# Overlapping weights of the dilated heads added before the ones matmuls, q and k loads moved ahead of half of the value loads, and the query and key copies of two batches moved

## The chip, the cores and the metric

The kernel runs on one core of one Trainium2 chip. The metric is the device time of one execution in microseconds (us), as the median of the runs taken. The engines named below are PE (TensorE, the matmuls), DVE (VectorE), ACT (ScalarE), POOL (GpSimd) and SP (SyncE); in this kernel POOL mostly issues the loads and SP mostly the transposing DMAs and the stores.

## What is computed

Windowed attention over 8 batches, 8 heads, 576 positions and 64 features, followed by a feed-forward layer over the 4608 tokens. Heads 0 to 3 ("near") look at the last 32 positions; heads 4 to 7 ("dilated") look at every fourth of the last 128.

```python
scores = q @ k.transpose(0, 1, 3, 2) / sqrt(64)
rel = pos[:, None] - pos[None, :]
near    = (rel >= 0) & (rel < 32)                        # heads 0..3
dilated = (rel >= 0) & (rel < 128) & (rel % 4 == 0)      # heads 4..7
attn = softmax(where(mask, scores, -1e9))
x = (attn @ v) laid out as [4608, 512]
h = maximum(x @ w_in, 0)          # [4608, 2048]
out = (h * h) @ w_out             # [4608, 512]
```

## The kernel before

**Groups.** The feed-forward layer is cut into 288 groups, numbered from 0. The first 64 groups do the first 1024 tokens in tiles of 256; after that each tile of 512 tokens has 32 groups. The first 16 groups of such a tile are the first layer (line 888: four matmuls of 512 columns each into one PSUM tile `pf`, which ACT then empties with a Relu at line 901 and DVE squares at line 902). The last 16 are the second layer (line 930, four matmuls a group, one `pf` tile for four groups, which ACT copies out at line 936). The pool `ps_f`, whose tiles are named `pf`, has four buffers; `ps_a` (`pa`) has two, `ps_o` (`po`) and `ps_d` (`pd`) one each.

**Attention between the groups.** The attention of later batches is put between the groups by a list that is written out by hand: entries (group, rank, batch, code), sorted by group and rank and carried out after that group. The engines run their instructions in program order, so this list sets the order on PE, ACT and DVE. Batch b is tied to group t = 32(b-1). The heads of a batch are taken as four pairs e = 0 to 3; e = 0 and 1 are near, e = 2 and 3 dilated. The codes are:

- R (line 475 on): DVE copies the 16 first and 16 last positions of the dilated heads of a batch into `ends`, which lies in the tile `kbd`; four codes, two copies each (lines 479 and 482).
- K and Q (lines 471 and 473): copies of keys into `k_both` (in `kbd`) and of queries into `q_both` (the tile `qT`); for batches 5 to 7 there are four K and four Q codes for e = 0 and as many for e = 1. A code that ends in "a" runs on ACT, any other on DVE.
- V: a *visit*, the function `quadrants`. It takes a list of pairs whose scores are wanted and a list of pairs whose softmax weights are ready, and issues all their matmuls (line 617) as 64 by 64 pieces, on the four quadrants of the PE array at once. Each piece goes to the quadrant (g, c): row half g, column half c. The order of issue is made by always taking from the quadrant that has the fewest columns so far.
- E: exponential of one half of a pair's scores on ACT (line 654), then the mask on DVE (line 656). For near pairs two adds (line 663) then put sums of overlapping columns into `sums`, in `kbd`.
- L and X: logarithm of the denominators (lines 630 and 631, or 635 and 636) and exponential of its negative (line 640) on ACT, then two multiplications on DVE that write the attention output `xT` (lines 643 and 645).

**One visit.** For each pair with weights there are the products with v (the list `P_` in the code) and the products with a block of ones (the list `D_`), which give the denominators. For a dilated pair each row half has 8 pieces of 80 and 2 of 64 columns in `P_` (768 columns), and 4 pieces of 160 and 2 of 64 in `D_` (768 columns). In `D_`, the two chunks x = 0 and 1 of a residue class cover positions 0 to 79 and 48 to 127, so they overlap in 48 to 79. For a near pair, a row half has 832 columns in `P_` and 608 in `D_`. Scores are 384 columns a quadrant for a dilated pair, and 448 or 384 for a near one.

With one pair, `P_` and `D_` of a row half lie in different quadrants. With two pairs (a *double* visit) `P_` and `D_` of one pair lie in the same quadrant, and the other pair has the other two quadrants. The second pair of a double visit takes two `pf` tiles for its outputs and denominators, and the second pair of scores takes two more.

Visits that hold a dilated pair's weights are these: group 59 (pairs 2 and 3 of batch 2 together), groups 71, 81 and 101 (one dilated pair each), and seven double visits with one near and one dilated pair, at groups 119, 143, 151, 175, 183, 207 and 215. For batch 6, whose t is 160, the visit at group 151 makes the scores of its pair 0; for batch 7 it is the visit at group 183.

**Loads.** POOL issues the loads in order. For batches 4 to 7 the order is: `load_v_rows(b, "d0")`, then four loads of q and k of batch b+1 (two of 320 KB, two of 256 KB), then `load_v_rows(b, "1")`. The "d" part is eight loads (the values of the dilated heads), "0" and "1" are eight loads of 18 KB each for the near pairs 0 and 1. The q and k tiles are then turned by four DMA transposes (line 238) from SP. A load of q into a staging tile waits until the transposes of the batch before have read it.

**Where the copies stand.** For batch 6 the R codes follow groups 134 to 137, the K and Q codes for pair 0 groups 137 to 143, all on DVE; for batch 7 it is 32 groups later. For batch 5 the R codes are at 109 to 112 and K and Q of pair 0 at 112 to 116, with Q on ACT.

Of the kernel before, what the change touches and what calls it, by code (L numbers as in the profile page):

```python
# [27 lines left out]
    "1o0 1o1f | 1a3 1Q0 | 1K0 1o3 | 1Q1 1K1 | 1Q2 | 1b0 | | 1Q3 1K2 L2:vwp L3:q00123 L3:q10123 L2:vwdr | L2:x | | "  # L28
    "2q0 | | 2k0 1V2 | 1b2 1p0 | 1b1 1V3 1K3 | L3:x | 1p2 1p1f | 2a0 1b3 | 2k1l 2b0 2o0 1p3f 2k1h | 2q1 | | 2p0 "
    "L3:Vd0 L4:q00123 L4:q10123 L3:V1 2a1 | 2b1 | | 2o1 | | | 2p1f | | | | L4:x | | | | | | | | | | | | | | | | | "  # L30
    "| L4:Vd0 L5:q10123 L5:q00123 L4:V1 | | | | | | | | | | | | | | | | L5:x | L5:Vd0 L6:q10123 L6:q00123 L5:V1"
)


# [29 lines left out]
def kernel(  # L64
# [258 lines left out]
    def scores(b: int, e: int, part: int):  # L323
        ps = ps_a.tile([P, 512], f32, name="pa")
        if part == 0:
            pts[e] = p_pool.tile([P, 832], bf16, name="pt")
        pt = pts[e]
        n = 0
        for i, r, m0, m1 in blocks(b, e, part):
            if r is None:  # L330
                w = RES * (m1 - m0)
                nc.tensor.matmul(  # L332
                    ps[:, n : n + w].rearrange("p (r m) -> p r m", r=RES),
                    kbd[:, e, i, :], qT[:, e, :, m0:m1], start=True, stop=True,
                )
            else:
                w = m1 - m0
                nc.tensor.matmul(ps[:, n : n + w], kbd[:, e, i, :], qT[:, e, r, m0:m1], start=True, stop=True)
            n += w
        off, mask = half_at(b, e)  # L340
        off *= part
        nc.scalar.activation(pt[:, off : off + n], ps[:, 0:n], ACT.Exp, scale=SCALE)
        nc.vector.tensor_tensor(
            out=pt[:, off : off + n], in0=pt[:, off : off + n],
            in1=mask[:, off : off + n], op=ALU.mult,
        )
# [138 lines left out]
            )  # L485

    sums = kbd[:, 3, 0:4, :].rearrange("p (e x) c -> p e (x c)", e=2)
    sp, op = {}, {}

    def byr(ap):  # L490
# [2 lines left out]
    def quadrants(scs, pvs):  # L493
# [14 lines left out]
        for n, (b, e) in enumerate(pvs):  # L508
# [11 lines left out]
            for g, rows in enumerate(sides):  # L520
# [9 lines left out]
                if not dil:  # L530

                    def blk(i):
                        y = 448 * (i % 2) + 96 * (i // 2)
                        return byr(w[:, y : y + (64 if i == 8 else 96)])

                    for x, i0, k in ((1, 1, 4), (0, 2, 3)):
                        for i in range(i0, i0 + 2 * k, 2):
                            P_.append((o4[:, :, 16 * i - 16 : 16 * i + 8], vrow(i), blk(i), 96))
                        y, m0 = 448 * x + 96 * (i0 // 2), 24 - 16 * x
                        to = d4.rearrange("p r (i m) -> p i r m", m=32)  # L540
                        mid = w[:, y : y + 96 * k].rearrange("p (i r m) -> p i r m", i=k, r=RES)
                        D_.append((to[:, 0:k, :, m0 : m0 + 8], one, mid[:, :, :, 8:16], 32 * k))
                        m0 = 16 * x
                        k = 4 - x
                        pairs = sums[rows, e, 128 * x : 128 * x + 32 * k].rearrange("p (i r m) -> p i r m", i=k, r=RES)
                        D_.append((to[:, 0:k, :, m0 : m0 + 8], one, pairs, 32 * k))
                    for i, ms, to, z in ((0, slice(16, 24), slice(0, 8), 32), (0, slice(0, 16), None, 64), (8, slice(0, 16), slice(112, 128), 64)):
                        P_.append((end if to is None else o4[:, :, to], vrow(i), blk(i)[:, :, ms], z))
                        if to is None or i:
                            D_.append((dend if to is None else d4[:, :, to], one, blk(i)[:, :, ms], z))  # L550
                    D_.append((d4[:, :, 112:120], one, blk(7)[:, :, 16:24], 32))
                else:
                    for x in range(2):
                        ms = slice(48 * x, 48 * x + 80)
                        for j in range(2):
                            y = 448 * (j ^ turn_)
                            piece = w[:, y : y + 320].rearrange("p (c m) -> p c m", c=2)[:, :, 80 * x : 80 * x + 80]
                            for c in range(2):
                                r = 2 * c + j
                                P_.append((o4[:, r, ms], vds[b][rows, e - NE // 2, x, D * r : D * r + D], piece[:, c, :], 80))  # L560
                            D_.append((d4[:, j::2, ms], one, piece, 160))
                    for i, j, to in ((0, 1, None), (8, 0, slice(112, 128))):
                        y = 448 * (j ^ turn_) + 320
                        P_.append((end if to is None else o4[:, :, to], vrow(i), byr(w[:, y : y + 64]), 64))
                        D_.append((dend if to is None else d4[:, :, to], one, byr(w[:, y : y + 64]), 64))
# [53 lines left out]
    def natural_step(b: int, code: str):  # L619
# [28 lines left out]
        else:  # L648
            g = int(code[2])
            if g == 0:  # L650
                pts[b, e] = p_pool.tile([P, 832], bf16, name="pt")
            n = 384 if e >= NE // 2 else (448, 384)[g]
            pt = pts[b, e][:, 448 * g : 448 * g + n]
            nc.scalar.activation(pt, sp[b, e][g][:, 0:n], ACT.Exp, scale=SCALE)  # L654
            mask = (mask_f if e >= NE // 2 else mask_n)[:, 0:n]
            nc.vector.tensor_tensor(out=pt, in0=pt, in1=mask, op=ALU.mult)  # L656
            if g and e < NE // 2:
                even, odd = (
                    pts[b, e][:, y : y + 384].rearrange("p (i r m) -> p i r m", i=4, r=RES) for y in (0, 448)
                )  # L660
                for x, one, two in ((0, even, odd), (1, odd[:, 0:3], even[:, 1:4])):
                    n = 4 - x
                    nc.vector.tensor_tensor(
                        out=sums[:, e, 128 * x : 128 * x + 32 * n].rearrange("p (i r m) -> p i r m", i=n, r=RES),
                        in0=one[:, :, :, 16:24], in1=two[:, :, :, 0:8], op=ALU.add,
                    )
# [19 lines left out]
    def first_step(code: str):  # L686
# [56 lines left out]
        elif what == "S":  # L743
# [2 lines left out]
                first["S", e, part] = pool.tile([P, 512], f32, name=nm)  # L746
            ps = first["S", e, part]
            if part == 0:
                pts[e] = p_pool.tile([P, 832], bf16, name="pt")
            bl = blocks(0, e, part)  # L750
            y = 0
            for x, (i, r, q0, q1) in enumerate(bl):
# [315 lines left out]
    for b in range(NATURAL, B):  # L1068
# [32 lines left out]
        else:  # L1101
# [9 lines left out]
                steps.extend((t + 27 + 2 * x, 1, b + 1, f"E2{x}") for x in range(2))  # L1111
            norm(3, t + 23)
            norm(1, t + 24)
        at = t - (14 if b < PAIRED else 19 if b == PAIRED else 26)
        for x, code in enumerate(("R00", "R01", "R10", "R11")):
            steps.append(((57, 57, 54, 55)[x] if early else at + x, 1, b, code))
        for x, code in enumerate(("K00", "K01", "K10", "K11", "Q00", "Q01", "Q10", "Q11")):
            if b < PAIRED:
                steps.append((t + x if early else t - 6 + x, 1, b, code))
            else:  # L1120
                if b > PAIRED:
                    steps.append((t - 23 + x - max(x - 4, 0) // 2, 1, b, code + "0"))
                else:
                    steps.append((t - 16 + x % 4 + x // 4, 3, b, code + "0" + "a" * (x // 4)))
                steps.append((t - 8 + x, 1, b, code + "1"))
    steps.sort(key=lambda x: x[:2])
    program = [x.split() for x in PROGRAM.split("|")]
# [2 lines left out]
    for g, group in enumerate(groups):  # L1130
        for b in [x for x in CROSS if CROSS[x] == g]:
            cross_all(b)
        for b in [x for x in LOAD_V if LOAD_V[x] == g]:
            load_v_rows(b, "d0")
            if b + 1 < B:
                for part in (1, 0):
                    load_qk(b + 1, part, [0, 1, 2, 3])
            load_v_rows(b, "1")
        group()
        for code in program[g + 1] if g + 1 < len(program) else ():  # L1140
            run(code)
# [32 lines left out]
```

## Time and profile before

| | us |
|---|---|
| median of 3 runs | 301.71 (301.47 to 301.91) |
| the profiled execution, whole | 302.44 |
| its span | 300.7 |
| PE busy | 293.0 (97%) |
| ACT busy | 196.3 (65%) |
| DVE busy | 166.2 (55%) |
| POOL busy | 129.2 (43%) |
| line 888, 704 matmuls | 128.6 |
| line 930, 592 matmuls | 129.9 |
| line 901, 144 Relus on ACT | 83.6 |
| line 902, 144 squares on DVE | 60.3 |
| line 656 with `mask_f`, 24 masks of dilated pairs | 8.2 |
| line 457, 80 loads on POOL | 43.6 |

The granted TensorE clock is 0.999 of full speed. How to read the views: in a timeline a line has the start in us, the time from the first start to the last end, the engine, the line of the kernel, the operation with its output and inputs, the shape, and the number of instructions merged into it. In the chain of waits a line has the start, the duration and the work that held the chain. The visits lie between stretches of lines 888 and 930 of that chain, so the wall time of a visit is the gap between two of these.

### The profile page before, as it was taken

The page shows a single profiled execution, that of the slowest core. Times are in us where ns is not written, and L with a number is a line of the kernel's source. Part 1 is how long each engine was busy: PE and PEld are TensorE (multiplying, and loading weights), DVE is VectorE, ACT ScalarE, POOL GpSimd, SP SyncE. Part 2 cuts the span into 40 slices and gives each one's busy share as a digit, 9 for nine tenths or more (in the row PEclk, how much of TensorE's full clock was granted, in tenths as well). Part 3 has the DMA queues.
Part 4 walks back from the last instruction along what each step waited for, and adds up shares of the span by engine and source line. Part 5 has one row for each costly group of instructions (what it writes and reads, how often), then busy time and mean ns, then how long its engine had stood idle before and what let it go on. Part 6 is the DMA issues. An engine that isn't in the chain of part 4 may idle for free.

```text
span 300.7 us, 7625 instructions
## 1 busy us (share of the span) xinstructions
PE 293.0 (97%) x3045; PEld 168.6 (56%) x3045; DVE 166.2 (55%) x491; ACT 196.3 (65%) x409; POOL 129.2 (43%) x210
## 2 busy tenths in 40 slices
PE   8889999999999999999999999999999999999994
PEld 3579856958855445554555455555555455445443
DVE  1666556998858655668649564866445235005300
ACT  6777748859977864789667676667567566226511
POOL 8579864393795954757765286200000000000000
PEclk9999999999999999999999999999999999999999
DMA  7999999999999959999999699202200200121022
GB/s 111 201 153 212 209 156 218 176 155 179 174 148 179 187 59 200 127 187 125 163 210 173 91 149 184 14 17 75 56 0 18 91 35 0 37 71 35 0 72 70
DMA packets 83123, 35.42 MB, mean 118 GB/s; under 512 B 52624, under 2 KB 78480, under 8 KB 83088
## 3 DMA queue, kind: packets, MB, share of 16 engines
q0 software_dynamic: 49280, 18.43, 55.0%
q1 hardware_dynamic: 33120, 16.18, 26.1%
q8 instruction: 24, 0.39, 0.5%
q10 hardware_dynamic: 688, 0.33, 0.5%
q14 instruction: 11, 0.09, 0.1%
HBM read 37.40 MB, written 9.44 MB: 156 GB/s over the span
## 4 chain that ended last, share of the span: by engine, by line
PE 91%; DMA 5%; ACT 1%; POOL 1%; issue 0%; ACTq 0%; POOLq 0%
PE pf L930 42%; PE pf L888 41%; DMA vd<-in_v_dram 3%; DMA kb<-in_k_dram 2%; PE po L617 2%; PE pf L617 1%; PE pa L258 1%; PE pa L617 1%; PE pd L617 1%; PE pa L332 1%; PE po L395 1%; PE pd L397 0%; POOL qb L171 0%; ACT h2T L901 0%; ACT rec L828 0%
## 5 line engine op out<-in xcount | busy, mean ns | idle before, releaser
L888 PE MATMUL pf<-xT,w_in 128*128 128x512 bf16 (+1 forms) x704 | 128.6, 341 | 1.7 <-ACT rec L828 1.3
L930 PE MATMUL pf<-w_out_sb,h2T 128*128 128x512 bf16 (+2 forms) x592 | 129.9, 374 | 0.0
L888 PEld LDWEIGHTS <-w_in 128*128 128x128 bf16 x704 | 77.7, 113 | 48.2 <-DMA w_in<-in_moe_w_in_dram 2.2
L901 ACT ACTIVATE h2T<-pf 128x512 bf16<-128x512 f32 x144 | 83.6, 599 | 30.1 <-PE pf L888 30.0
L902 DVE TENSOR_TENSOR h2T<-h2T 128x512 bf16<-128x512 bf16 x144 | 60.3, 425 | 61.3 <-ACT h2T L901 59.1
L930 PEld LDWEIGHTS <-h2T 128*128 128x128 bf16 x592 | 55.4, 98 | 61.3 <-issue 0.3
L457 POOL DMA_DIRECT2D vbd<-in_v_dram x80 | 43.6, 562 | 24.9 <-DMA kb<-in_k_dram 5.8
L936 ACT COPY osb<-pf 128x512 f32<-128x512 f32 (+1 forms) x36 | 20.7, 574 | 50.3 <-PE pf L930 47.3
L192 POOL DMA_DIRECT2D vbd<-in_v_dram x16 | 10.9, 689 | 11.9 <-DMA kb<-in_k_dram 4.5
L171 POOL DMA_DIRECT2D qb<-in_q_dram x18 | 12.9, 718 | 6.8 <-DMA xx<-qb 3.9
L640 ACT ACTIVATE rec<-rec 128x576 f32<-128x576 f32 x22 | 15.0, 682 | 0.6
L654 ACT ACTIVATE pt<-pa 128x384 bf16<-128x384 f32 (+1 forms) x26 | 11.8, 496 | 4.5 <-DVE xT L645 2.7
L444 POOL DMA_DIRECT2D vd<-in_v_dram x20 | 12.2, 623 | 5.4 <-PE pf L617 4.8
L643 DVE TENSOR_TENSOR xT<-po,rec 128x512 bf16<-128x512 f32 x13 | 9.0, 692 | 9.5 <-ACT rec L640 9.2
L171 POOL DMA_DIRECT2D kb<-in_k_dram x18 | 12.7, 707 | 1.0 <-DMA vd<-in_v_dram 1.0
L449 POOL DMA_DIRECT2D vbd<-in_v_dram x20 | 12.0, 619 | 1.3 <-DMA vbd<-in_v_dram 1.2
L656 DVE TENSOR_TENSOR pt<-pt,mask_n 128x448 bf16<-128x448 bf16 (+1 forms) x20 | 7.1, 373 | 9.2 <-ACT pt L654 9.1
L656 DVE TENSOR_TENSOR pt<-pt,mask_f 128x384 bf16<-128x384 bf16 x24 | 8.2, 355 | 6.2 <-ACT pt L654 6.1
L643 DVE TENSOR_TENSOR xT<-pf,rec 128x512 bf16<-128x512 f32 x9 | 6.2, 692 | 7.4 <-ACT rec L640 7.2
L471 DVE COPY qT<-xx 64x576 bf16<-64x576 bf16 (+1 forms) x28 | 10.0, 356 | 0.6
L617 PEld LDWEIGHTS <-vbd 64*64 64x64 bf16 x248 | 6.8, 107 | 3.8 <-issue 3.3
L473 DVE COPY kbd<-xx 64x320 bf16<-64x320 bf16 (+3 forms) x32 | 8.3, 260 | 0.6
(139 smaller groups left out, 320.9 us busy)
## 6 DMA issues: line engine op xcount, KB each, us to landing
qb<-in_q_dram POOLq DMA_DIRECT2D x7, 320.0 KB, 6.8
kb<-in_k_dram POOLq DMA_DIRECT2D x7, 320.0 KB, 8.1
vd<-in_v_dram POOLq DMA_DIRECT2D x32, 64.0 KB, 6.2
w_in<-in_moe_w_in_dram POOLq DMA_DIRECT2D x4, 512.0 KB, 8.2
w_out_sb<-in_moe_w_out_dram POOLq DMA_DIRECT2D x4, 512.0 KB, 12.7
out_dram<-osb SPq DMA_DIRECT2D x16, 128.0 KB, 4.0
qb<-in_q_dram POOLq DMA_DIRECT2D x7, 256.0 KB, 8.4
kb<-in_k_dram POOLq DMA_DIRECT2D x7, 256.0 KB, 9.0
```

The lines of the kernel that those rows point to most:

```text
L171: nc.gpsimd.dma_start(t[0:n, part, hs, :], src[b, hs, t0 : t0 + RES * n, :].rearrange("h (p r) d -> p h (r d)", r=RES))
L444: nc.gpsimd.dma_start(vds[b][rows, e, :, :], v[b, H // 2 + 2 * e + hl, 0:512, :].rearrange("(m p r) d -> p m (r d)", p=64, r=RES),)
L457: nc.gpsimd.dma_start(v_rows[b % 2][p0 + 16 * r : p0 + 16 * r + 16, e, :, :], v[b, 2 * e + hl, :, :].rearrange("(i m r) d -> r m i d", r=R ...
L617: nc.tensor.matmul(out, lhs, rhs, start=begin, stop=True, skip_group_check=True)
L640: nc.scalar.activation(rec[:, :], rec[:, :], ACT.Exp, scale=-1.0)
L643: nc.vector.tensor_tensor(out=tok[:, :, 16:M], in0=byr(o[:, :]), in1=byr(rec[:, 0:512]), op=ALU.mult)
L656: nc.vector.tensor_tensor(out=pt, in0=pt, in1=mask, op=ALU.mult)
L888: nc.tensor.matmul(to, w_in_sb[piece][:, kt, c0 : c0 + 509 : 4], rhs, start=(kt == kts[0] and x == 0), stop=(kt == kts[-1] and x == per - ...
L901: nc.scalar.activation(hv, acc[u][:, :].rearrange("p (x n) -> p x n", x=per), ACT.Relu)
L902: nc.vector.tensor_tensor(out=hv, in0=hv, in1=hv, op=ALU.mult)
L930: nc.tensor.matmul(cur[m][:, c0:c1], h2[:, f, P * m : P * m + P], w_out_sb[:, f, c0:c1], start=(f == 0), stop=(f == NF - 1),)
L936: (nc.vector.tensor_copy if last and part == 1 else nc.scalar.copy)(osb[:, c0:c1], cur[m][:, c0:c1])
```

## The change

For dilated pairs the overlap is added once, after the masks, by one DVE instruction a pair (128 columns), into a place `shared` in `kbd`. The ones matmuls of such a pair then have, in each row half and for each j, pieces of 96, 64 and 96 columns in place of two of 160: 640 columns in 8 matmuls instead of 768 in 6. The weights tile `pt` grows from 832 to 896 columns. In the loads the "0" part moves behind the q and k loads. The codes R, and K and Q for pair 0, of batch 6 move three groups later, those of batch 7 four groups; K and Q follow each other more closely, with Q on ACT and with the last rank of their group. For batch 6 the Q codes for pair 0 now follow groups 141, 142, 143 and 144; for batch 7 groups 174, 175, 176 and 177.

```diff
-    "L3:Vd0 L4:q00123 L4:q10123 L3:V1 2a1 | ...
-    "| L4:Vd0 L5:q10123 L5:q00123 L4:V1 | ... | L5:x | L5:Vd0 L6:q10123 L6:q00123 L5:V1"
+    "L3:Vd0 L4:q00123 L4:q10123 L3:V1 2a1 | ...
+    "| L4:Vd L5:q10123 L5:q00123 L4:V01 | ... | L5:x | L5:Vd L6:q10123 L6:q00123 L5:V01"
...
+    shared = kbd[:, 3, 4:6, :].rearrange("p e (x c m) -> p e x c m", x=2, c=2)
...
+                    for j in range(2):
+                        y = 448 * (j ^ turn_)
+                        both = w[:, y : y + 320].rearrange("p (c m) -> p c m", c=2)
+                        for m0, m1, rhs in (
+                            (0, 48, both[:, :, 0:48]),
+                            (48, 80, shared[rows, e - NE // 2, j ^ turn_]),
+                            (80, 128, both[:, :, 112:160]),
+                        ):
+                            D_.append((d4[:, j::2, m0:m1], one, rhs, 2 * (m1 - m0)))
                     for x in range(2):
                         ms = slice(48 * x, 48 * x + 80)
                         for j in range(2):
...
-                            D_.append((d4[:, j::2, ms], one, piece, 160))
...
-                pts[b, e] = p_pool.tile([P, 832], bf16, name="pt")
+                pts[b, e] = p_pool.tile([P, 896], bf16, name="pt")
...
+            if g and e >= NE // 2:
+                z = pts[b, e][:, :].rearrange("p (x y) -> p x y", x=2)[:, :, 0:320].rearrange("p x (c m) -> p x c m", c=2)
+                nc.vector.tensor_tensor(
+                    out=shared[:, e - NE // 2], in0=z[:, :, :, 48:80], in1=z[:, :, :, 80:112], op=ALU.add
+                )
...
-        at = t - (14 if b < PAIRED else 19 if b == PAIRED else 26)
+        at = t - {PAIRED: 19, PAIRED + 1: 23, PAIRED + 2: 22}.get(b, 14)
...
-                if b > PAIRED:
-                    steps.append((t - 23 + x - max(x - 4, 0) // 2, 1, b, code + "0"))
-                else:
-                    steps.append((t - 16 + x % 4 + x // 4, 3, b, code + "0" + "a" * (x // 4)))
+                steps.append((at + 3 + x % 4 + x // 4, 3, b, code + "0" + "a" * (x // 4)))
                 steps.append((t - 8 + x, 1, b, code + "1"))
...
-            load_v_rows(b, "d0")
+            load_v_rows(b, "d")
             if b + 1 < B:
                 for part in (1, 0):
                     load_qk(b + 1, part, [0, 1, 2, 3])
-            load_v_rows(b, "1")
+            load_v_rows(b, "01")
```

## The prediction

> **What bounds the kernel now.** I read the page's chain by engine first, then the chain of waits from 150 us on, then the visits one by one in the timelines of PE, ACT and DVE.
>
> ```profile
> PE 91%; DMA 5%; ACT 1%; POOL 1%; issue 0%; ACTq 0%; POOLq 0%
> ```
>
> The DMA share lies in the first 21 us, ahead of any changed line. After that PE holds the chain almost without a break:
>
> ```profile
> 150.86 13.81 PE pf L888 x64
> 165.89 7.01 PE pf L930 x32
> ...
> 226.62 7.01 PE pf L930 x32
> 234.44 7.02 PE pf L930 x32
> ```
>
> Two things are to be seen. 64 matmuls of 512 columns take 13.81 us, 0.42 ns a column. And visits are gaps in this list: group 143's lasts from 164.67 to 165.89, 1.22 us, group 215's from 233.63 to 234.44, 0.81 us. So the time changes by what the visits' matmuls save, plus every new moment in which PE stands; idle time of ACT and DVE counts for nothing until it reaches PE.
>
> **Columns saved.** In the visit at group 59 both pairs are dilated, and the ones matmuls follow each other so:
>
> ```profile
> 85.01 0.23 PE L617 MATMUL pd<-pt,mk 64*64 64x160 bf16 x2
> ...
> 85.04 0.20 PE L617 MATMUL pa<-pt,mk 64*64 64x64 bf16 x2
> 85.07 0.23 PE L617 MATMUL pd<-pt,mk 64*64 64x160 bf16 x2
> ...
> 85.14 0.23 PE L617 MATMUL pd<-pt,mk 64*64 64x160 bf16 x2
> ```
>
> Starts are 0.07 us apart after 160 columns and 0.03 after 64: time goes by columns, and the quadrants run side by side. All four quadrants have 128 columns less here: 128 x 0.42 = 0.054 us. In the seven mixed double visits the dilated pair's quadrants hold 1536 columns and the near pair's 1440; to this come the scores, 832 and 768, where the heavier half falls on g = 0 for both. The longest quadrant is then 2368 before (at 0.42 ns 0.99 us of the 1.22 us seen, the rest being the change between the big array and quadrants). After, the dilated quadrants fall to 2240 and the near ones, at 2272, decide: 96 columns, 0.040 us, also where no scores follow (1536 to 1440). Seven times 0.040 is 0.28. In groups 71, 81 and 101 the ones matmuls lie beside value products of 768 columns, which stay: nothing. Sum -0.34 us. Bounds: 0, if the four added matmuls a pair eat it, and -0.50, if the three single visits gain 0.054 each too. I take -0.34, because the spacing above is proportional down to 64 columns and no new piece is smaller.
>
> The Trainium skill, TensorEngine Tiling (Array Packing), section Performance Considerations, speaks against this part: it gives each matmul an overhead of about 60 cycles, and says that one column costs as much as 60. Read as an addition, two more matmuls a row half would take back 120 of the 128 columns and leave the sum near 0; the 0.03 us that the trace shows from one 64-column piece to the next has no room for it, and read as a floor it touches no piece here.
>
> **The DVE adds.** The change puts 12 on DVE, of 128 columns. The nearest row is line 663, two adds of 128 and 96 columns that start after the mask they wait for:
>
> ```profile
> 144.43 0.34 DVE L663 TENSOR_TENSOR kbd<-pt 128x128 bf16<-128x128 bf16 x2
> ```
>
> That is 0.17 us each. An add also breaks the overlap of masks: four take 1.23 us in a row, 0.31 each, one alone 0.36. So 0.17 to 0.25 us a pair. For ten of the twelve pairs DVE has time: the mask of pair 2 of batch 5, for one, ends near 149.7, and its visit is at 164.67. At group 59 it has not:
>
> ```profile
> 83.19 1.23 DVE L656 TENSOR_TENSOR pt<-pt,mask_f 128x384 bf16<-128x384 bf16 x4
> ...
> 84.97 0.30 DVE L482 COPY kbd<-xx 64x128 bf16<-64x128 bf16 x1
> ```
>
> ```profile
> 85.35 0.32 PE L617 MATMUL pa<-xx 64*64 64x80 bf16 x16
> 85.49 0.20 PE L617 MATMUL pa<-kbd 64*64 64x64 bf16 x4
> ```
>
> Both adds stand between these masks and batch 3's R copies, whose last ends at 85.27; the scores from `kbd` at 85.49 (85.44 after the saving) read them. The slack is 0.17 us, and the copies come 0.34 to 0.50 later: PE stands 0.17 to 0.33 us, and a little more if the second pair's mask, now near 84.7, is late for the first value products at 84.69. I take +0.30; bounds 0 (DVE catches up) and 0.45.
>
> **Q copies on ACT ahead of the visits.** A visit with two pairs and two score pairs takes all four `pf` tiles: the last tile of the first layer, that of group 143, becomes the denominators of the second pair. Its release is the Relu:
>
> ```profile
> 163.85 0.60 ACT L901 ACTIVATE h2T<-pf 128x512 bf16<-128x512 f32 x1 [0.27 <-PE pf L888]
> 164.71 0.60 ACT L901 ACTIVATE h2T<-pf 128x512 bf16<-128x512 f32 x1 [0.27 <-PE pf L888]
> 165.21 0.92 ACT L654 ACTIVATE pt<-pf 128x448 bf16<-128x448 f32 x2
> ```
>
> ```profile
> 165.36 0.19 PE L617 MATMUL pf<-pt,mk 64*64 64x64 bf16 x1
> ```
>
> The Relu ends at 165.31, and 0.05 us later PE writes that tile: no slack. ACT takes a Relu every 0.86 us and is free 0.36 of it (0.50 from one start to the next when they follow directly, as 164.71 and 165.21 show). A Q copy on ACT is this row of batch 5's:
>
> ```profile
> 140.04 0.67 ACT L471 COPY qT<-xx 64x576 bf16<-64x576 bf16 x1
> 140.61 0.57 ACT L936 COPY osb<-pf 128x512 f32<-128x512 f32 x1
> ```
>
> 0.57 us to the next instruction (0.67 at most), so each copy pushes ACT back by 0.21 to 0.31. Two (groups 141, 142) stand ahead of the Relu of 143: it comes 0.42 to 0.62 later, and everything behind that matmul on PE's queue, the other ones pieces, the scores and the second layer, waits. Batch 7 has one copy (group 174) ahead of the same spot at group 175, where the Relu ends at 195.78 and PE writes at 195.82: 0.21 to 0.31. Less a sliver of slack, I take +0.40 and +0.20; lower bound 0 for both, if ACT fits the copies in.
>
> **The next visit.** The other two Q copies lie on ACT between a visit and the release of `po`, which the next visit writes first. At 175 to 183 the last DVE read of `po` starts at 201.06 and lasts 0.69, with the visit at 203.37: 1.6 us of slack. Three copies now stand on that ACT chain (175, 176, 177), 1.7 us, on top of the 0.20 by which it starts late; PE is 0.20 late too. Following the chain (second pair's exponential 0.77 later, its DVE product, the masks' exponentials that wait for that product, then two copies and the next logarithm), the product from `po` ends near 203.7 and PE wants it at 203.53: +0.18, bounds 0 and 0.55. At 143 to 151 only two copies lie there, and it fits with 0.2 us to spare: 0, at most 0.10. Batch 5's copies, which do not move, show the kind: ACT ends them at 142.56 and the visit at 142.52 lasts 1.33 us instead of 1.22.
>
> **Loads and R.** R, K and Q on DVE are covered by PE and cost nothing either way; without that cover the four DVE Q copies were 0.31 each. The q load of batch 6 waited 1.88 us at 135.78 for batch 5's transposes; now POOL reaches it 6.6 us earlier (without the 4.43 of eight loads and the 2.19 that they waited), waits there longer, and the eight loads behind it queue. Who is late: the rows of near pair 0. Batch 5's issue (16 loads of 0.54 from 138.57, and the waits of 3 us seen between them) now ends near 150, and the visit that reads them is at 164.67; batch 6's end near 173, read at 195.14. Over 12 us of cover, so 0; without the cover, up to a landing of 4.0 us. Earlier transposes help no PE wait that the trace has.
>
> **Sum.** -0.34 + 0.30 + 0.40 + 0.20 + 0.18 = +0.74 us. The profiled execution took 302.44 (span 300.7), 0.73 over the median of the runs, so such an execution would take 303.18; on the median, 301.71 + 0.74 = 302.45. All bounds together reach from -0.50 to +2.03 (0.45 + 0.62 + 0.31 + 0.55 + 0.10, with nothing saved).
>
> **Rivals.** *The stalls don't come* (not slower): ACT or DVE absorb what I put on them and only the columns remain, 301.71 - 0.34 = 301.37. For it: the copies leave DVE, whose masks and products then run sooner, and 0.2 us of slack in three places would do. Against: Relu and write lie 0.05 us apart in two visits. It decides if the Relu of group 143 still starts within 0.1 us of its matmul. *ACT stays behind*: copies at 0.67, `po` late at 151 and 183 at their bounds: 0.30 + 0.62 + 0.31 + 0.10 + 0.45 - 0.34 = +1.44, 303.15. For it: batch 5's stall. *Value rows late*: up to the 4.0 us of one landing, 305.7; against it the 12 us of cover. *The change doesn't do what it says*: the single visits could gain as well, which is the -0.50 bound.
>
> **How the numbers follow.** Forecast 0.57, with its own range 302.1 to 302.9; no stalls 0.25; ACT behind 0.15; value rows 0.03. The range is 301.3 to 303.2: it leaves out the rows and the far ends of the second and third case. 0.2%, about what a measurement of this kernel can tell from no change, is 0.6 us: slower from 302.31, faster below 301.11. Of the forecast two thirds are slower by that, 0.37, the rest within; ACT behind and rows add 0.18; of the no-stall case, whose sum is 0.1% but whose unseen help on DVE may add, 0.10 is faster and 0.15 within. Slower 0.55, same 0.35, faster 0.10.
>
> **What would show it.** In the changed profile: the double visits without Q copies ahead (groups 119, 151, 207, 215) shorter by 0.04 us; group 143's visit near 1.6 us and 175's near 1.4, with ACT's Relus late behind `qT` copies; a gap at the first `po` write of group 183; `pa<-kbd` late in group 59. If the mixed visits keep their length, the columns were not the limit; if 143's stays at 1.2 us, the forecast falls to the no-stall case.

## The result and the profile after

The changed kernel takes 304.03 us (median of 6 runs, 303.38 to 305.96); the kernel before took 301.59 us beside it (6 runs, 301.37 to 301.91). The ratio is 1.0092, with a 95% interval of 1.0063 to 1.012: slower by 0.6 to 1.2%. The forecast was 302.45, with a range up to 303.2. The direction was right, the size was not: +0.74 us had been summed up, and +2.44 came.

The profiled execution of the changed kernel took 304.05 us (span 302.3, granted clock 1.0). The page's share of the chain by engine is the first thing to look at:

```profile
PE 79%; DMA 9%; ACT 3%; POOL 3%; DVE 2%; issue 2%; SPq 0%; ACTq 0%; POOLq 0%
```

PE has lost 12 points. Not all of that is time: the chain is followed back from releaser to releaser, and one step of it is wrong, as will be seen. The stretch that answers to the end of the list shown of before is this, from the chain of waits of the changed kernel (start, duration, what held the chain):

```profile
194.72 0.47 issue
195.19 0.66 ACT qT L471
...
197.76 0.68 ACT qT L471
198.45 0.69 ACT rec L649
...
200.92 0.67 ACT qT L471
201.60 0.60 ACT rec L639
...
202.34 0.68 ACT qT L471
203.03 0.69 ACT rec L649
203.75 0.69 DVE xT L652
204.44 0.14 DVE xT L654
204.58 0.20 PE po L626
204.78 0.19 issue
204.97 0.19 PE po L626
...
206.21 7.01 PE pf L944 x32
213.22 13.81 PE pf L902 x64
...
236.03 7.03 PE pf L944 x32
```

Between groups 174 and 183 the chain has left PE for ACT, and four of its steps there are Q copies (`qT`, line 471). The undisturbed visits still lie between stretches of the two big lines: group 215's first matmul starts at 235.25 in this chain and the big ones go on at 236.03, 0.78 us, where before it took 0.81.

To see where the time went I measured each visit with its neighbourhood: from the first full-size matmul after one visit to the first full-size matmul after the next, and took the difference to the profile of the kernel before. The table has these differences in us for all profiles of this study ("total": all intervals from behind the visit of group 56 to behind that of group 215).

| kernel | 59 | 119 | 143 | 151 | 175 | 183 | 207 + 215 | total |
|---|---|---|---|---|---|---|---|---|
| changed | +.71 | +.06 | +.49 | +.38 | -.04 | +1.08 | -.03 | +2.53 |
| changed, again (e11) | +.62 | +.08 | +.49 | +.31 | -.04 | +1.08 | -.03 | +2.40 |
| changed, batch 2 as before (e12) | 0 | +.06 | +.49 | +.33 | -.05 | +1.00 | -.03 | +1.70 |
| later copies alone (e1) | +.18 | +.04 | +.51 | +.35 | -.03 | +.98 | 0 | +1.93 |
| adds alone (e2) | +.28 | +.05 | -.02 | -.01 | -.23 | -.02 | -.04 | +.03 |
| loads alone (e3) | +.01 | +.04 | 0 | 0 | +.81 | 0 | 0 | +.76 |
| changed, Q on DVE (e4) | +.20 | +.08 | -.02 | +.03 | -.23 | -.02 | -.03 | -.10 |
| changed, Q early on ACT (e5) | +.30 | +.07 | +.26 | +.07 | +.05 | -.01 | -.04 | +.59 |
| copies alone, batch 7 earlier (e6) | 0 | -.01 | +.52 | +.41 | +.30 | +.30 | 0 | +1.41 |
| adds alone, from batch 3 (e7) | 0 | -.01 | -.02 | -.01 | -.23 | -.02 | -.04 | -.37 |
| e7 with fewer ones pieces (e8) | +.01 | -.01 | -.02 | -.02 | +.27 | -.02 | -.04 | +.13 |
| copies alone, waits taken early (e9) | 0 | 0 | +.51 | +.02 | -.02 | +.60 | 0 | +1.38 |
| copies alone, scores first (e10) | +.01 | -.01 | +.51 | +.36 | -.03 | +.71 | 0 | +1.44 |

Visits repeat to a few hundredths, so most rows can be compared by eye. Two things in the table are not the kernels' doing. In the profile of before PE paused for 0.2 us in the second layer behind group 151 (at 176.65), and in most others it did not, so -.23 in the column of 175 stands for "no change" (0.21 for the pause, 0.02 for the columns); the last section comes back to this pause. And in all profiles but those of before and of the changed kernel the records of 29 matmuls are missing: the page of e11 has 3064 matmuls to 3093 weight loads, that of the changed kernel, the same program, 3093 of both. Where a record is missing the chain of waits shows a short "issue" that was none. One of the 29 is the first full-size matmul behind group 56, which starts the measured stretch 0.23 us late, so the totals of those rows have 0.23 added.

Four visits hold nearly all of the loss: 59, 143, 151 and 183. ACT at group 143, in the timeline of the changed kernel:

```profile
162.71 0.60 ACT L915 ACTIVATE h2T<-pf 128x512 bf16<-128x512 f32 x1 [0.27 <-PE pf L902]
163.20 0.66 ACT L471 COPY qT<-xx 64x576 bf16<-64x576 bf16 x1
163.76 0.59 ACT L915 ACTIVATE h2T<-pf 128x512 bf16<-128x512 f32 x1
164.38 0.67 ACT L471 COPY qT<-xx 64x576 bf16<-64x576 bf16 x1
164.96 0.59 ACT L915 ACTIVATE h2T<-pf 128x512 bf16<-128x512 f32 x1
```

And PE there, and at group 183:

```profile
165.59 0.19 PE L626 MATMUL pf<-pt,mk 64*64 64x64 bf16 x1 [0.32 <-ACT h2T L915]
...
204.58 0.20 PE L626 MATMUL po<-pt,vbd 64*64 64x96 bf16 x1 [0.66 <-DVE xT L654]
204.97 0.19 PE L626 MATMUL po<-pt,vbd 64*64 64x64 bf16 x1 [0.19 <-issue]
```

The last Relu of the first layer starts at 164.96, 0.63 us after the visit's first matmul at 164.33 (before: 164.71, 0.11 us after it); the write of the tile that it empties follows its end (165.55) at 165.59. At 183 PE stands 0.66 us for the product that reads `po`, and then, which no step of the prediction has, the second `po` matmul comes 0.39 us after the first. In the profile of before the two start within 0.02 us, and one line of PE holds both:

```profile
203.30 0.23 PE L617 MATMUL po<-pt,vbd 64*64 64x96 bf16 x2
```

### The profile page after: what moved, and what is told of

The parts are those of the page before. It is cut to its first block, busy times and chain, and to the rows that moved or that the text cites. A ratio compares the mean times of both kernels' runs of the same rounds, so it can differ in the third digit from the quotient of the medians.

```text
span 302.3 us, 7734 instructions
## 1 busy us (share of the span) xinstructions
PE 293.2 (97%) x3093; PEld 168.5 (56%) x3093; DVE 165.7 (55%) x495; ACT 201.6 (67%) x417; POOL 128.9 (43%) x210
## 4 chain that ended last, share of the span: by engine, by line
PE 79%; DMA 9%; ACT 3%; POOL 3%; DVE 2%; issue 2%; SPq 0%; ACTq 0%; POOLq 0%
PE pf L944 36%; PE pf L902 36%; DMA kb<-in_k_dram 5%; DMA w_in<-in_moe_w_in_dram 3%; PE po L626 1%; POOL vbd L457 1%; PE pa L258 1%; ACT qT L471 1%; POOL qb L171 1%; DMA out_dram<-osb 1%; PE pf L626 1%; PE pa L626 1%; DMA vbd<-in_v_dram 1%; ACT pt L663 1%; PE pa L332 1%
## 5 line engine op out<-in xcount | busy, mean ns | idle before, releaser
L626 PE MATMUL po<-pt,vbd 64*64 64x96 bf16 (+2 forms) x170 | 8.2, 201 | 1.0 <-DVE xT L654 0.7
```

What stands on the lines that cost most here:

```text
L626: nc.tensor.matmul(out, lhs, rhs, start=begin, stop=True, skip_group_check=True)
```

## The experiments

The first four take the change apart.

**e1, later copies alone.** The kernel before with only this part of the change:

```diff
-        at = t - (14 if b < PAIRED else 19 if b == PAIRED else 26)
+        at = t - {PAIRED: 19, PAIRED + 1: 23, PAIRED + 2: 22}.get(b, 14)
...
-                if b > PAIRED:
-                    steps.append((t - 23 + x - max(x - 4, 0) // 2, 1, b, code + "0"))
-                else:
-                    steps.append((t - 16 + x % 4 + x // 4, 3, b, code + "0" + "a" * (x // 4)))
+                steps.append((at + 3 + x % 4 + x // 4, 3, b, code + "0" + "a" * (x // 4)))
```

> The kernel before with the moved copies alone (R, K, Q of pair 0 of batches 6 and 7, Q on ACT). Theory: the ACT copies make PE stand in the visits of groups 143, 151, 175 and 183, which in the two profiles grew by 0.49, 0.38, 0.17 and 1.09 us, 2.13 in all (2.2 with the ones matmuls at their old length): 303.8 us against 301.6. Rival (the loads): the chain of the changed kernel names a load of value rows ahead of group 151's visit, so without the new order of loads that visit keeps its 1.21 us and the time is at most 303.3.

Measured: 303.55 us against 301.89, ratio 1.0057 (1.004 to 1.0075). The losses at 143, 151 and 183 are all there, +0.51, +0.35 and +0.98.

**e2, the adds alone.** The changed kernel with the copies and the loads put back:

```diff
-        at = t - {PAIRED: 19, PAIRED + 1: 23, PAIRED + 2: 22}.get(b, 14)
+        at = t - (14 if b < PAIRED else 19 if b == PAIRED else 26)
...
-            load_v_rows(b, "d")
+            load_v_rows(b, "d0")
```

> The kernel before with the adds and the shorter ones matmuls alone. Theory: group 59's visit grows from 0.99 to about 1.7 us because batch 3's R copies come late behind the two adds, the seven mixed visits shrink by 0.02 to 0.04 each: +0.7 - 0.2 = +0.5, 302.1 us. Rival: batch 3's R copies were late for another reason (the loads issued by POOL beside them), then group 59 keeps about 0.95 us and the time is 301.4.

Measured: 301.81 us against 301.89, ratio 0.9998 (0.9987 to 1.0008). DVE in the timeline of this kernel, at group 59:

```profile
83.82 0.23 DVE L668 TENSOR_TENSOR kbd<-pt 128x128 bf16<-128x128 bf16 x1
...
84.06 0.32 DVE L482 COPY kbd<-xx 64x128 bf16<-64x128 bf16 x1
...
84.50 0.30 DVE L482 COPY kbd<-xx 64x128 bf16<-64x128 bf16 x1
```

An add (line 668) takes 0.23 us, two stand ahead of the R copies, and group 59 loses 0.28. Each mixed visit but that at 119 gains some 0.02.

**e3, the loads alone.** The kernel before with the three lines of the load order changed:

```diff
-            load_v_rows(b, "d0")
+            load_v_rows(b, "d")
...
-            load_v_rows(b, "1")
+            load_v_rows(b, "01")
```

> The kernel before with the new order of loads alone. Theory: no change, 301.6 within 0.3; the visits keep their lengths. Rival (the loads): the visit of group 151 grows by 0.4 us, because the value rows come behind the q and k loads, 302.0 or more.

Measured: 302.24 us against 301.89, ratio 1.001 (0.9997 to 1.0023): not told from no change. No visit is longer. The only loss in its profile is one pause of 0.86 us in the second layer, where no attention stands:

```profile
173.51 2.54 PE pf L930 x11
176.04 0.86 issue
176.91 4.26 PE pf L930 x19
```

**e4, Q copies on DVE.** The changed kernel, with Q of batches 6 and 7 at its new places but on DVE:

```diff
-                steps.append((at + 3 + x % 4 + x // 4, 3, b, code + "0" + "a" * (x // 4)))
+                steps.append((at + 3 + x % 4 + x // 4, 3, b, code + "0" + "a" * (b == PAIRED and x // 4)))
```

> The changed kernel with the Q copies of batches 6 and 7 back on DVE, at their new places. Theory: the visits of groups 143, 151, 175 and 183 fall to 1.20 us and only group 59 is left: 301.6 + 0.69 - 0.16 = 302.1 us. Rival (the later places, not ACT): R, K and Q at their later groups are late on DVE too, a visit stays above 1.3 us and the time stays above 303.

Measured: 301.85 us against 301.89, ratio 1.0007 (0.9993 to 1.0021). 143, 151 and 183 lose nothing (-0.02, +0.03, -0.02). The places do no harm, the engine does.

**e5, Q copies early on ACT.** The changed kernel with these copies on ACT, after four groups in a row, 136 to 139 and 168 to 171, ahead of the visits at 143 and 175:

```diff
-                steps.append((at + 3 + x % 4 + x // 4, 3, b, code + "0" + "a" * (x // 4)))
+                y = at + 3 + x % 4 + x // 4 if b == PAIRED or x < 4 else t - 24 + x % 4
+                steps.append((y, 3, b, code + "0" + "a" * (x // 4)))
```

> The changed kernel with the Q copies of batches 6 and 7 still on ACT, but after groups 136 to 139 and 168 to 171, so that four Relus lie between the last copy and the visit. Theory (place, not engine): ACT has caught up before the visits, those of groups 143, 151, 175 and 183 fall back to 1.20 us, 301.9 us like with Q on DVE. Rival (ACT has too much to do in all): the backlog only moves, at least one of the four visits stays 0.2 us longer and the time stays above 302.8.

Measured: 302.44 us against 301.82, ratio 1.0016 (0.9995 to 1.0037). 183 is whole again (-0.01), 151 nearly (+0.07), but 143 still loses 0.26 (and 175 0.28, from the -0.23 that no change has there to +0.05). ACT in the timeline of this kernel:

```profile
161.47 0.67 ACT L471 COPY qT<-xx 64x576 bf16<-64x576 bf16 x1
162.16 0.60 ACT L915 ACTIVATE h2T<-pf 128x512 bf16<-128x512 f32 x1
162.78 0.67 ACT L471 COPY qT<-xx 64x576 bf16<-64x576 bf16 x1
163.47 2.06 ACT L915 ACTIVATE h2T<-pf 128x512 bf16<-128x512 f32 x4
```

From one Relu to the next with a copy between them it is 1.30 us (160.86 to 162.16) and 1.31 (162.16 to 163.47), while PE delivers a tile every 0.86. After four such copies four Relus stand in line (2.06 us for four) when the visit comes: the places were too close together for the backlog to be worked off.

**e6, batch 7 one group earlier.** The copies alone (e1), with batch 7's one group earlier, so that two Q copies stand ahead of the visit at 175 and two behind it, in place of one and three:

```diff
-        at = t - {PAIRED: 19, PAIRED + 1: 23, PAIRED + 2: 22}.get(b, 14)
+        at = t - {PAIRED: 19, PAIRED + 1: 23, PAIRED + 2: 23}.get(b, 14)
```

> The moved copies alone, with those of batch 7 one group earlier, so that two Q copies stand ahead of group 175's visit and two between it and group 183's, as batch 6 has them. Theory (each visit grows by the copies ahead of it on ACT): group 175 grows by 0.5 instead of 0.17, group 183 by 0.35 instead of 1.0, so 0.3 us less in all than with the copies alone, 303.2 to 303.3 us. Rival (group 183 is late for another reason, its own loads or keys): it keeps 1.0 us, and the time is 303.8.

Measured: 303.12 us against 301.82, ratio 1.0036 (1.0017 to 1.0056). The loss at 175 goes from -0.03 to +0.30, that at 183 from +0.98 to +0.30. One copy less on the chain to 183 is worth 0.68 us there and costs 0.33 ahead of 175: batch 7 now looks like batch 6: with the 0.21 of the pause in before, its visit at 175 loses 0.51 (143: 0.52), and that at 183 0.30 (151: 0.41).

**e7 and e8, the adds from batch 3 on, and fewer pieces.** e7 is e2 with group 59 as before; e8 also takes only two pieces of 128 columns for each j, and leaves the overlapping weights out of the denominators.

```diff
-                    for j in range(2):
+                    for j in range(2 if b != XB else 0):
...
+                            if b == XB:
+                                D_.append((d4[:, j::2, ms], one, piece, 160))
...
-            if g and e >= NE // 2:
+            if g and e >= NE // 2 and b != XB:
```

```diff
-                            (0, 48, both[:, :, 0:48]),
-                            (48, 80, shared[rows, e - NE // 2, j ^ turn_]),
-                            (80, 128, both[:, :, 112:160]),
+                            (0, 64, both[:, :, 14:78]),
+                            (64, 128, both[:, :, 96:160]),
```

> The adds and shorter ones matmuls alone, but not for batch 2, whose visit at group 59 keeps the old form (two pieces of 160). Theory: group 59 keeps about 0.95 us, the mixed visits shrink by 0.02 each, 301.5 to 301.7 us: not slower than before. Rival: the adds cost elsewhere, and the time is 302 or more.

> As the run before it, but the ones matmuls of a dilated pair are two pieces of 128 columns for each j instead of 96, 64 and 96: the same 640 columns in 6 matmuls instead of 8; the overlapping weights are left out of the denominators. Asked: why the mixed visits gain only 0.02 us where 96 columns are 0.04. If the two added matmuls a row half take the other half, these visits shrink by a further 0.02 us; if the near pair's quadrants decide, they keep their length.

Measured: e7 301.68 us against 301.82, ratio 0.9989 (0.9971 to 1.0007), not told from the kernel before; group 59 is at 0. e8, 302.15 us in its one run: the mixed visits gain the same 0.02 as with three pieces. So the two more matmuls a row half are not what took back the other 0.02 of the 0.04 forecast; what did stays open.

Two questions were left: why the second `po` matmul starts late, and what belongs to group 59.

**e9, the waits taken early.** In a double visit the weight loads of the first two `po` matmuls carry, beside the wait for DVE, four waits each for the loads of the near pair's values: eight loads, eight semaphores. e9 is e1 with one 16-column matmul at groups 148 and 180 that reads those values and so does the eight waits there:

```diff
                 cur[m] = ps_f.tile([P, DM], f32, name="pf")
+                if m == 1 and tk0 in (2048, 2560):
+                    near1 = v_rows[(tk0 // NT + 1) % 2][:, 1, 1, 0:16]
+                    nc.tensor.matmul(cur[m][:, 0:16], mk[:, 256 + P : 256 + 2 * P], near1, start=True, stop=True)
```

> This is the kernel of e1 (later copies alone), plus one small matmul of 16 columns at the start of the second-layer tile of groups 148 and 180, which reads the values of near pair 1 of batches 5 and 6, so that PE takes the eight waits for their loads there; its output is overwritten by the first matmul of the tile. In e1 the second po matmul of the visits at 151 and 183 starts 0.31 to 0.33 us after the first one, with nothing named but issue. Theory (PE works off the waits for the loads, which stand on the weight loads of the first two po matmuls, only after the late release by DVE; the loads themselves landed 20 us before): the second po matmul now starts within 0.1 us of the first, the intervals after the visits at 151 and 183 change by about +0.05 and +0.70 against the kernel before, in place of +0.35 and +0.98, and the small matmuls cost up to 0.1 us each; the whole is near +1.2 us (ratio 1.004). Rival (the pause belongs to a PE that has stood idle, or to the other waits): the 0.3 us stay, intervals +0.35 and +0.98, ratio 1.006.

Measured: 302.98 us against 301.89, ratio 1.0029 (1.0014 to 1.0045). 151 falls from +0.35 to +0.02, 183 from +0.98 to +0.60. PE at group 151, first in e1, then in e9 (both from the timeline):

```profile
172.75 0.42 PE L617 MATMUL po<-pt,vbd 64*64 64x96 bf16 x2
172.99 0.38 PE L617 MATMUL pf<-qT,kbd 64*64 64x96 bf16 x17
```

```profile
173.07 0.23 PE L617 MATMUL po<-pt,vbd 64*64 64x96 bf16 x2
173.08 0.39 PE L617 MATMUL pf<-qT,kbd 64*64 64x96 bf16 x17
...
204.14 0.23 PE L617 MATMUL po<-pt,vbd 64*64 64x96 bf16 x2 [0.53 <-DVE xT L643]
204.15 0.39 PE L617 MATMUL pf<-qT,kbd 64*64 64x96 bf16 x17
```

The two `po` matmuls together last 0.42 us in e1 and 0.23 in e9, and the scores follow 0.24 us after the first one in e1 and 0.01 after it in e9. At 151 DVE's last read of `po` (line 643) ends at 172.61 in e1 and at 172.94 in e9, 0.14 and 0.13 us before the first `po` matmul: the release is equally late, only the waits are gone. This is the theory's outcome, and it shows that the waits for eight loads that landed long ago cost 0.33 (151) and 0.38 us (183) of the visit when they come after a late release. The pause in e1 was smaller than its expectation put it, 0.23 us between the two `po` matmuls (0.42 for both, less 0.19 for one); the rest is lost behind the second.

**e10, scores first.** e1 with the scores of the next batch ahead of the first `po` matmuls in the visits at 151 and 183:

```diff
-                items[1:1] = two
+                y = pvs[0] in ((PAIRED, 1), (PAIRED + 1, 1))
+                items[1 - y : 1 - y] = two
```

> This is the kernel of e1 (later copies alone), with the scores of the next batch's pair 0 put ahead of the first po matmuls in the visits at 151 and 183; the same matmuls in another order. Theory (what these visits lose is the late release of po and the waits that are worked off after it, both hidden by work that needs neither): the scores fill some 0.3 us, so the interval at 151 falls from +0.35 to about 0, and that at 183 from +0.98 to +0.3 to +0.65, the whole from +1.70 to some +0.7 to +1.0 us (ratio 1.003). Rival (the scores are late too, since the last Q copy on ACT is what holds the visit): the intervals stay at +0.35 and +0.98.

Measured: 303.22 us against 301.89, ratio 1.005 (1.0031 to 1.007). Half of the theory's outcome: 183 falls to +0.71, since the scores fill a part of the wait for `po`, but 151 stays at +0.36. At 151 the first `po` matmul now starts at 172.50, after the scores, and the next one at 172.86:

```profile
172.26 0.39 PE L618 MATMUL pf<-qT,kbd 64*64 64x96 bf16 x18
172.50 0.19 PE L618 MATMUL po<-pt,vbd 64*64 64x64 bf16 x1
172.63 0.22 PE L618 MATMUL pa<-xx 64*64 64x80 bf16 x2
172.86 0.20 PE L618 MATMUL po<-pt,vbd 64*64 64x96 bf16 x1
```

DVE's last read of `po` ended at 172.15, 0.35 us ahead of that first matmul, and the waits still show: in the trace they start at 172.29, behind the first scores. What held them until then isn't shown, so this run doesn't say how early the release has to come. In the profile of before that read ended at 171.25, 1.59 us ahead of the first `po` matmul at 172.84, and nothing showed.

**e11, the changed kernel again, and e12, the changed kernel with batch 2 as before.** The edit of e12 is e7's, on the changed kernel.

> The changed kernel once more, beside the two others. Theory: visits at 143, 151, 175 and 183 lose +0.5, +0.4, 0 to +0.2 and +1.1 as in its first profile, since these are set by program order; ratio 1.008 to 1.010. Group 59: if the +0.71 of the first profile is the adds' doing, it comes again (R copies of 0.55 us); if the two adds cost only what e2, e4 and e5 show (+0.20 to +0.30) and the rest was the state of that one execution, it is +0.2 to +0.3 here.

> The changed kernel with batch 2 (group 59) as before: no adds and the old ones pieces there, all else changed. The two profiles of the changed kernel lose 0.71 and 0.62 us at group 59, those with the adds alone or without Q on ACT only 0.20 to 0.30. Theory (the loss at 59 comes through the two adds ahead of the R copies; that the R copies then take 0.55 instead of 0.30 us adds to it): the interval after 59 is 0 if the R copies take 0.30 us and about +0.2, as in e1, if they take 0.55; the whole is +1.5 to +2.0 us, ratio 1.006 to 1.007 against 1.009 for the whole change. Rival (the loss at 59 belongs to the rest of the change, its loads or its longer R copies): +0.4 or more stays there and the ratio stays at 1.008 to 1.010. Visits at 143, 151, 175 and 183 as in the changed kernel by both: +0.5, +0.35, 0 and +1.1.

Measured: e11 304.57 us against 301.89, ratio 1.0096 (1.0068 to 1.0124), with +0.62 at group 59 and the other visits as in the first profile. e12 303.68 us against 301.65, ratio 1.0063 (1.004 to 1.0087), with 0 at group 59 and +0.49, +0.33 and +1.00 at 143, 151 and 183. The intervals of the two ratios overlap a little; by the profiles the loss at 59 goes away with batch 2's adds. But the R copies took only 0.29 and 0.39 us in e12, so it doesn't say what slow copies cost alone. e1 does: no adds, copies of 0.51 and 0.52 us, and +0.18. DVE and PE at that place, in e11's timeline:

```profile
84.25 0.23 DVE L668 TENSOR_TENSOR kbd<-pt 128x128 bf16<-128x128 bf16 x1
...
84.50 0.47 DVE L482 COPY kbd<-xx 64x128 bf16<-64x128 bf16 x1
...
85.09 0.56 DVE L482 COPY kbd<-xx 64x128 bf16<-64x128 bf16 x1
```

```profile
85.70 0.22 PE L626 MATMUL pa<-kbd 64*64 64x64 bf16 x4 [0.41 <-DVE kbd L482]
```

The copies behind the adds are slower than in e2 (0.47 and 0.56 us where e2 has 0.32 and 0.30), and PE waits for the last one. What slows them is open: the changed kernel had it in both profiles and e1 too, e4, e5, e6, e10 and e12 had 0.29 to 0.40. The Trainium skill (SBUF — State Buffer, section Who interferes with whom) says that a DVE copy in its two-port mode and GpSimd share a pair of ports, which the one that starts first holds for its whole instruction. POOL does issue q and k loads beside the slow copies; but it issues the same loads beside the 0.30 us copies of e4, so these runs do not show that rule at work.

## Why the prediction was right or wrong

**What bounds the kernel, and the direction: right.** The loss is new moments in which PE stands, at visits, and the three visits 143, 151 and 183 lose it through the Q copies on ACT: there with the copies alone (e1), gone with the same copies on DVE (e4).

**Columns, -0.34: half of it.** The mixed visits that no copy touches are 0.02 us shorter, not 0.04 (207, 215, and 143 to 183 in e2 and e7). Group 119's is no help: it differs by -0.01 to +0.08 between kernels, with and without adds. At 0.02 the sum over seven is -0.14 instead of -0.28. The overhead of added matmuls, the bound at 0, is not the reason (e8). What group 59 gained can't be separated from its stall.

**Group 59, +0.30 less its own columns (0.054), about +0.25 net: the step was right, the copies behind it were mis-sized.** e2, e4 and e5 have +0.20 to +0.30. In the changed kernel it is +0.71 and +0.62, since the R copies behind the adds were taken at the 0.30 us that before showed and took up to 0.56. The two parts can be put together as an estimate: the scores are 0.37 to 0.47 us late by the adds alone (the loss and the 0.17 of slack) and 0.35 by slow copies alone (e1, 0.18 and the same slack), which makes a loss of 0.55 to 0.65 when the slack is taken off once.

**Groups 143 and 175, +0.40 and +0.20: right.** Less the columns that makes +0.36 and +0.16; measured +0.49, and, with the 0.21 us of the pause in the profile of before, +0.17. A copy between two Relus costs what was said here: from 163.20 to 163.76, 0.56 us, and from 164.38 to 164.96, 0.58. The lower bound of 0 (ACT fits the copies in) is out.

**Group 183, +0.18: the term that failed most, +1.08.** Place and mechanism were named, its size was not. Two things were too small. First, the price of a copy: 0.57 us to the next instruction is right at 163.20 and 164.38, but each of the three copies of this chain took 0.68 to 0.69 (197.76 to 198.45, 200.92 to 201.60, 202.34 to 203.03): 2.06 us for three instead of 1.7. The prediction had seen 0.67 "at most" and took the lower price here. What decides between the two is open. It is not the instruction that follows: in e5 a Relu starts 0.69 us behind two copies (161.47, 162.78), and in the profile of before an exponential 0.58 behind a copy of batch 5 (138.76).

Second, what comes behind the release of `po`. The release itself was read rightly, at the end of the large product:

```profile
203.75 0.69 DVE L652 TENSOR_TENSOR xT<-po,rec 128x512 bf16<-128x512 f32 x1 [1.96 <-ACT rec L649]
204.35 0.21 DVE L654 TENSOR_TENSOR xT<-pa,rec 128x64 bf16<-128x64 f32 x1
```

The views name the small product (line 654) as PE's releaser, but it reads `pa`, and in the trace PE's wait is over at 204.48, 0.04 us after the large product's end (204.44) and before the small one's (204.56). From the release to the first `po` matmul it is still 0.14 us (0.06 in e9). These 0.14 and the 0.36 of the copies are 0.50, against the 0.48 by which the wait of 0.66 us exceeds the forecast 0.18. Then the second `po` matmul is late as well.

**The waits behind a late release: not in the prediction at all.** They are 0.38 of the loss at 183 (e9 against e1) and the whole of the loss at 151, which had been put at 0 to 0.10 because `po` would be free "with 0.2 us to spare". It was free: its last read ended at 172.96 and PE's first `po` matmul started at 173.10. But the prediction counted slack up to that matmul, as if PE began work at that point. Most of these waits are instructions of their own on PE's sequencer, behind the wait for the release. This is where those of the visit at 151 start, before and in the changed kernel (view of the visits' line; number, duration in ns, first and last start):

```profile
L617 PEldq EVENT_SEMAPHORE  x3: 51/51/51, 171.3 to 171.5; - x3
```

```profile
L626 PEldq EVENT_SEMAPHORE  x3: 51/51/51, 173.0 to 173.3; - x3
```

Before, they are done during the matmuls ahead of the visit, 1.3 us before its first `po` matmul; in the changed kernel they lie in the visit. Of the eight waits for loads two are over by 169.1 in both, and six come behind the release. e9 takes these waits elsewhere, and 151 costs +0.02. The rival *ACT stays behind* had `po` late at both visits, with copies at 0.67, and was the nearest case; it too lacked this step, and stopped at 303.15 (303.25, had its sum taken the prediction's own bound of 0.55 at 183 in place of 0.45).

**Loads at 0, R and K at 0: held.** e3 shows no visit longer, and its ratio is not told from 1. The chain of waits of the changed kernel does name a load at 151:

```profile
167.90 3.62 POOL vbd L457 x7
171.51 0.06 issue
171.57 1.85 DMA vbd<-in_v_dram
173.42 0.17 PE po L626
```

That is the wrong step mentioned above. The loads issued at 167.90 bring batch 6's values; those that this visit reads, batch 5's, were issued by 145.2. The same 0.35 us came with the old load order (e1), and the waits alone, worked off earlier, remove it (e9). The two sets of loads share their semaphores, and a load named as the last releaser was here only the last semaphore that PE got round to. The rival *value rows late* is out.

**The sum.** By their own parts the runs give +1.66 us for the copies, -0.08 for the adds and +0.35 (an interval that holds 0) for the loads, 1.9 together against 2.44 for the whole. The remainder of 0.5 is within the noise of these sums (the interval of e1 alone is 0.5 us to either side); 0.2 of it can be seen at group 59, which loses 0.71 and 0.62 in the changed kernel and 0.18 and 0.28 in e1 and e2.

No version here beats the kernel before for certain: the best, e7, is at 0.9989 with an interval that holds 1.

## What to carry to other kernels

Slack on a chain counts up to the first instruction that the late event blocks, and everything that the engine would have done ahead of time behind it (waits on semaphores that have long been signalled, above all) is added once the slack is gone; ask for the release to come well ahead (here 1.59 us was enough and 0.14 was not), or let an earlier instruction do those waits. Where an instruction shows two prices, add up a chain with the higher one as well: the copy cost 0.57 us in one place and 0.69 in another, and on the chain that mattered it was 0.69 three times. An engine that is 65% busy on average has no room in the last stretch before a visit, and the same copies on the engine that was not on that chain cost nothing.

## What the runs showed of the hardware that was not expected

The waits for eight loads that had landed some 20 us before cost PE 0.33 to 0.38 us where the release ahead of them came 0.14 to 0.15 us before the first `po` matmul (e1 against e9, at 151 and 183). They cost nothing that shows where it came 1.59 us before (before) or where another matmul had done them (e9: 0.01 us from the first `po` matmul to the scores). As an estimate it is some 0.06 us for each of the six that come behind the release (0.33 and 0.38 over six). The Trainium skill (Perfetto Trace Analysis, section Per-engine timelines) describes how the sequencer pushes a TensorE instruction into a wait queue and goes on to decode the next one. The profile of before agrees: PE's sequencer is at the waits of the visit at 171.3 to 171.5, while the first matmul of the visit starts at 172.84.

In three profiles PE pauses once, with nothing named but issue, in the second layer behind group 151: from one matmul's start to the next it is 0.42 us in before (at 176.65), 1.24 in e3 (175.67, the 0.86 shown above) and 0.72 in e8 (176.14), where it is 0.22 otherwise. The cause is open. In e3 a packet of the queue named "instruction" moved shortly before, from 174.38 to 175.44, but in e2 one moved from 174.16 to 175.04, and no pause followed. Such a pause shifts an interval by as much as the smaller terms of this study.
